# x's two halves, the weights' VectorE steps and row 0 put at other places of the attention loop of a fused attention and two-layer kernel

## The chip, the core and the metric

One core of a Trainium2 chip runs the whole kernel as one program. Its engines work side by side, each on its own queue of instructions, strictly in the order in which they were written: TensorE (PE, with its weight loads as PEld), VectorE (DVE), ScalarE (ACT), GpSimd (POOL) and SyncE (SP), which issues the loads. They wait for one another through semaphores. The metric is the device time of one execution in microseconds; lower is better.

## The reference

```python
def _attn_ref(q, k, v):
    scores = scale * np.matmul(q, k.transpose(0, 1, 3, 2))
    scores = np.where(mask, -1000000000.0, scores)
    scores = scores - np.max(scores, axis=-1, keepdims=True)
    attn = np.exp(scores)
    attn = attn / (np.sum(attn, axis=-1, keepdims=True) + 1e-09)
    return np.matmul(attn, v).astype(np.float32)
...
x = np.ascontiguousarray(attn_out.transpose(0, 2, 1, 3)).reshape(B * S, H * D)
x = _moe_ref(x=x, **moe_kwargs)          # (sigmoid(x @ w_gate) * (x @ w_val)) @ w_out
return _moe2_ref(x=x, **moe2_kwargs)     # h = x @ w_in; (h * cos(h)) @ w_out
```

Causal attention with 2 batches, 12 heads, 448 positions and 64 columns per head; then two dense layers on 896 tokens of 768 columns, with 1536 and 2048 inner columns. The weights come as 64-bit floats, and the kernel makes 32-bit words of them on the chip.

## The kernel before

**Precision.** Each operand of the dense layers is kept as a high part and a low part (the rest), and a product is made of three matmuls: high by high, high by low, low by high. A high part is a ScalarE copy, the low part a VectorE subtraction behind it.

**The attention loop** runs over 12 pairs of heads, t = 0 to 11, and is a pipeline over three or four iterations. In iteration t stand, in the order in which they are written:

- `scores(t)`: for each of seven rows of 64 positions, in `ORDER = (0, 2, 1, 3, 4, 6, 5)`, the score matmuls on TensorE (L328) into a bank of PSUM, a score step on VectorE that masks and takes the extreme (L334, with a short read of its accumulator), and an exponential on ScalarE (L338) that also sums. The widths are 64 to 448 columns; the last row in this order has 384. At the end, from iteration 3 on, `next(preparing)` puts one step of the first weight chunk behind: `prepare()` makes the words (L182 on ScalarE, L184 on VectorE) and the high and low part (L193 on ScalarE, L195 on VectorE) in halves of 384 columns. VectorE's four steps of it fall into iterations 7, 8, 10 and 11, ScalarE's into 4, 5, 9 and 10.
- `attend(t - 2, t - 3)`: products with the values (L379), the first half for pair t - 2, the second for t - 3, whose x is then complete in PSUM.
- `transposes(t - 1, iteration(t))`: 14 transposes of the scaled exponentials (L353) in four groups g = 0 to 3, each into a bank and from there to SBUF by a copy of rows: groups 0 and 2 by VectorE (L360), 1 and 3 by ScalarE (L358). `iteration(t)` gives a hook, `before(g)`, that is called ahead of each copy.

**In the hook** stand, for the iterations from 3 on: ahead of the copy of group 1 the high part of x of pair t - 3 (`split_x(t - 3, 0)`, L392, ScalarE); ahead of that of group 2 `normalise(t)`: the reciprocals of the sums (`invert`, L297 and L298, VectorE) and the scaling of the seven rows by POOL (`scale`, L307), row 0 first; ahead of that of group 3 the low part of x (`split_x(t - 3, 1)`, L395, VectorE, from PSUM and the high part) and POOL's addition of both parts (L396). VectorE executes an iteration therefore as: seven score steps, weight step if there is one, first copy, reciprocals, second copy, low part of x.

**What sets the order.** The schedule is manual: the order in which the lines run is the order on each engine. PSUM has eight banks that all these tiles share, so the score matmuls of an iteration wait for the exponentials, copies and x's low part of the iteration before, whose banks they take over. The scaled rows live in three buffers.

**Behind the loop** the first dense product (L245 to L247) is woven with the last products and transposes; a full weight step of 768 columns (`decode_chunk`) and the high and low parts of x of pairs 9 to 11 stand there. The dense layers follow (L562 to L564 and others) until the end.

Of the kernel before, what the change touches and what calls it, by code (L numbers as in the profile page):

```python
# [10 lines left out]
F32 = mybir.dt.float32  # L11
# [7 lines left out]
ALU = mybir.AluOpType  # L19
# [4 lines left out]
NPAIR = H // 2  # L24
NQT = S // D
# [57 lines left out]
def attn_moe_moe2(  # L83
# [9 lines left out]
    nc = tc.nc  # L93
# [13 lines left out]
    def bank():  # L107
        return psum.tile([P, 512], F32, tag="ps", name="ps")
# [8 lines left out]
    XB = [[None] * KX for b in range(B)]  # L117
# [83 lines left out]
    def decode_chunk():  # L201
        c = step("decode")
        if c is not None:
            singles[c] = Chunk(c)
            for n in range(2):
                singles[c].decode(n, 0, singles[c].n)
# [11 lines left out]
    def prepare():  # L218

        step("split")  # L220
        k = Chunk(step("decode"))
        a, b = (0, k.n // 2), (k.n // 2, k.n)
        for todo in (
            [], [(k.decode, 0, a)], [(k.decode, 0, b)], [], [(k.decode, 1, a)],
            [(k.decode, 1, b)], [(k.split, 0, a)],
            [(k.split, 1, a), (k.split, 0, b)], [(k.split, 1, b)],
        ):
            for do, n, cols in todo:
                do(n, *cols)
            yield  # L230

    def decode_load():
        decode_chunk()
# [6 lines left out]
    def products(ps, wt, rhs, first, last, ks=None):  # L240
        hi, lo = wt
        n = len(rhs)
        for k in ks or range(n):
            r, blk = rhs[k], slice(k * P, k * P + P)
            mm(ps[:, :S], lhsT=hi[:, blk], rhs=r[:, 0], start=first and k == 0, stop=False)  # L245
            mm(ps[:, :S], lhsT=hi[:, blk], rhs=r[:, 1], start=False, stop=False)  # L246
            mm(ps[:, :S], lhsT=lo[:, blk], rhs=r[:, 0], start=False, stop=last and k == n - 1)  # L247
# [5 lines left out]
    with tc.tile_pool(name="apool", bufs=1) as apool, tc.tile_pool(name="a2", bufs=2) as a2:  # L253
# [46 lines left out]
        def scale(t, rows, engine):  # L300
            pb, (sums, rs) = pbuf[t % 3], soft[t]
            for i in rows:
                row, by = pb[:, POFF[i] : POFF[i] + D * (i + 1)], rs[:, i : i + 1]
                if engine is nc.scalar:
                    nc.scalar.activation(row, row, AF.Copy, scale=by)
                else:
                    engine.tensor_scalar(row, row, by, 1.0, op0=ALU.mult, op1=ALU.mult)  # L307

        def normalise(t, i0, i1):
            invert(t, i0, i1)  # L310
            scale(t, range(i0, i1), nc.gpsimd)

        def scores(t):

            blocks = at.pop(t).rearrange("p (n c) -> p n c", c=QKW)
            pb = pbuf[t % 3]
            nm = a2.tile([P, 8], F32, tag="nm", name="nm")
            sums = a2.tile([P, 8], F32, tag="sums", name="sums")
            soft[t] = sums, a2.tile([P, 8], F32, tag="rs", name="rs")
            for n, i in enumerate(ORDER):  # L320
                w = D * (i + 1)
                ps = bank()
                for h in range(2):
                    rows = slice(h * D, h * D + D)
                    o, k0 = ((1 - h) * D, 2 * D) if i in CROSSED else (h * D, D)
                    parts = ((i, i + 1, 0), (0, i, D)) if i == TURNED else ((0, i + 1, 0),)
                    for n0, n1, c in parts:
                        mm(  # L328
                            ps[o : o + D, c : c + (n1 - n0) * D], lhsT=blocks[rows, i, :D],
                            rhs=blocks[rows, n0:n1, k0 : k0 + D], start=n0 == parts[0][0], stop=True,  # L330
                            skip_group_check=True,
                        )
                m0 = S - D if i == TURNED else S - w
                nc.vector.tensor_tensor_reduce(  # L334
                    out=ps[:, :w], in0=ps[:, :w], in1=mask[:, m0 : m0 + w], scale=-0.125, scalar=3.0e38,
                    op0=ALU.add, op1=ALU.min, accum_out=nm[:, i : i + 1],
                )
                nc.scalar.activation(  # L338
                    pb[:, POFF[i] : POFF[i] + w], ps[:, :w], AF.Exp, scale=-1.0,
                    bias=nm[:, i : i + 1], accum_out=sums[:, i : i + 1],  # L340
                )
                if (t, n) in ROWS_BEHIND:
                    normalise(*ROWS_BEHIND[t, n])
            next(preparing, None)
# [43 lines left out]
        def split_x(t, part):  # L388
            b, p = divmod(t, NPAIR)
            x = XB[b][p]  # L390
            if part == 0:
                nc.scalar.activation(x[:, 0], xps[t][:, :S], AF.Copy)  # L392
            else:
                xf = x.bitcast(F32)
                nc.vector.tensor_tensor(x[:, 1], xps.pop(t)[:, :S], xf[:, 0], op=ALU.subtract)  # L395
                nc.gpsimd.tensor_tensor(X32[p][:, b], xf[:, 0], xf[:, 1], op=ALU.add)  # L396

        def iteration(t):

            def before(g):  # L400
                if g == 1 and t >= 3:
                    split_x(t - 3, 0)
                if t == 1 and g > 1:
                    normalise(1, *((0, 4), (4, NQT))[g - 2])
                if 1 < t < NP - 1 and g == 2:
                    normalise(t, 0, NQT)
                if t == NP - 1 and g == 2:
                    invert(t, 0, NQT)
                    scale(t, (1, 2, 3), nc.gpsimd)
                if t >= 3 and g == 3:  # L410
                    split_x(t - 3, 1)
            return before


# [4 lines left out]
        for t in range(NP):  # L419
            if t == 3:  # L420
                preparing = prepare()
            scores(t)
            if t + 3 < NP:
                load_attn(t + 3, (nc.sync,) * 2, [(0, VOFF)] if t else [(0, 4 * QKW), (4 * QKW, VOFF)])
            if t >= 2:
                attend(t - 2, *([t - 3] if t > 2 else []))
            if t + 3 < NP:
                load_values(t + 3)
            if t >= 1:
                transposes(t - 1, iteration(t))  # L430
            if t == NP - 1:
                scale(t, (4, 5), nc.scalar)
                scale(t, (6, 0), nc.vector)
            if t in (1, 2, 9):
                load_chunk()
# [3 lines left out]
        xr = [[XB[b][k] for k in KORD] for b in range(B)]  # L439
        products(pg[0], wt, xr[0], True, False, range(0, 2))  # L440
        attend(NP - 2, NP - 3)
        decode_chunk()
        transposes(NP - 1, iteration(NP))
        products(pg[0], wt, xr[0], False, False, range(2, 4))
# [2 lines left out]
        nc.scalar.copy(fence, xps[NP - 1][:, D : D + 1])  # L447
        split_x(NP - 2, 0)
        split_x(NP - 2, 1)
        products(pg[0], wt, xr[0], False, True, range(4, KX))  # L450
        attend(NP - 1)
        split_x(NP - 1, 0)
        split_x(NP - 1, 1)
        pg.append(bank())
        products(pg[1], wt, xr[1], True, True)

# [858 lines left out]
```

## Time and profile before

| what | us |
|---|---|
| median of 3 runs | 526.16 (526.01 to 526.53) |
| the profiled execution's own time | 525.88 |
| its span, first to last instruction | 524.1 |
| TensorE busy | 518.0 |
| VectorE busy | 433.5 |
| ScalarE busy | 354.7 |
| POOL busy | 57.4 |

The granted TensorE clock was 0.999 of full speed over the span. A busy time is the sum of an engine's instructions, with waits left out, but a matmul's end is modelled, so TensorE's busy share says little about its pace. The views that the next sections use are the timeline of an engine (start and length of each instruction, in us from the start of the span, and in brackets the idle time ahead of it with what ended it) and tables of groups of instructions.

### The profile page before, as it was taken

What the parts mean: (1) busy time and instruction counts of PE and PEld (TensorE: products, weight loads), DVE (VectorE), ACT (ScalarE), POOL (GpSimd) and SP (SyncE); (2) the same over time, 40 slices, a digit from 0 to 9 for tenths busy, and PEclk for the clock granted to TensorE, in tenths of its full rate; (3) what the DMA queues carried; (4) which work ended last, traced back from release to release, by engine and by line L of the source; (5) the groups of instructions that cost most, each with busy time, mean ns of one, the idle gap of its engine ahead of it and who ended that gap; (6) DMA issues with size and microseconds to landing.
All of it is one profiled execution on the core that took longest, in us unless ns stands there. A gap on an engine that the chain in (4) does not pass through costs nothing.

```text
span 524.1 us, 8771 instructions
## 1 busy us (share of the span) xinstructions
PE 518.0 (99%) x3252; PEld 469.3 (90%) x3252; DVE 433.5 (83%) x823; ACT 354.7 (68%) x694; POOL 57.4 (11%) x111
## 2 busy tenths in 40 slices
PE   8999999999999999999999999999999999999997
PEld 6776789999999999999999999999999999999996
DVE  7889969987777899988865779998899878896883
ACT  7998965675555676776645557776687967874550
POOL 5787740000000000000000000000000000000111
PEclk9999999999999999999999999999999999999999
DMA  8966014354444433323342413444333333353422
GB/s 300 393 209 218 2 61 131 111 165 137 127 127 132 135 120 123 120 83 121 88 154 82 159 61 120 128 151 143 123 121 100 104 98 101 100 161 120 157 88 88
DMA packets 15658, 68.98 MB, mean 132 GB/s; under 512 B 1824, under 2 KB 2848, under 8 KB 15616
## 3 DMA queue, kind: packets, MB, share of 16 engines
q1 hardware_dynamic: 14688, 65.72, 38.4%
q0 software_dynamic: 640, 2.29, 1.2%
q8 instruction: 25, 0.41, 0.3%
q10 hardware_dynamic: 288, 0.41, 0.2%
q14 instruction: 17, 0.14, 0.1%
HBM read 65.67 MB, written 2.75 MB: 131 GB/s over the span
## 4 chain that ended last, share of the span: by engine, by line
PE 86%; DVE 5%; ACT 5%; issue 3%; POOL 1%; DMA 0%; DVEq 0%; POOLq 0%; ACTq 0%
PE ps L563 18%; PE ps L564 18%; PE ps L562 18%; PE ps L245 8%; PE ps L247 8%; PE ps L246 8%; ACT pbuf L338 3%; PE ps L379 2%; PE ps L328 2%; PE ps L353 2%; DVE wf L184 1%; DVE ps L334 1%; PE ps L275 1%; ACT up L182 1%; DVE wlo L475 1%
## 5 line engine op out<-in xcount | busy, mean ns | idle before, releaser
L182 ACT ACTIVATE up<-wraw 128x768 f16<-128x768 bf16 (+2 forms) x71 | 74.2, 1045 | 0.0
L184 DVE SCALAR_TENSOR_TENSOR wf<-wraw,up 128x768 uint32<-128x768 uint32 (+2 forms) x71 | 68.2, 961 | 7.1 <-ACT up L182 5.4
L563 PE MATMUL ps<-T,whi 128*128 128x448 f32 x189 | 68.6, 363 | 0.0
L562 PE MATMUL ps<-T,whi 128*128 128x448 f32 x189 | 68.5, 363 | 0.0
L564 PE MATMUL ps<-T,wlo 128*128 128x448 f32 x189 | 68.2, 361 | 0.0
L529 ACT ACTIVATE whi<-s 128x768 fp32r<-128x768 f32 x46 | 38.9, 845 | 39.0 <-DVE s L475 38.9
L475 DVE TENSOR_TENSOR wlo<-s,whi 128x768 fp32r<-128x768 f32 x46 | 43.9, 955 | 12.2 <-ACT whi L529 11.6
L1170 POOL DMA_DIRECT2D out_dram<-sg x8 | 4.5, 568 | 430.3 <-DVE sg L1169 430.3
L245 PE MATMUL ps<-g,whi 128*128 128x448 f32 x120 | 43.6, 363 | 0.0
L247 PE MATMUL ps<-g,wlo 128*128 128x448 f32 x120 | 43.5, 362 | 0.0
L246 PE MATMUL ps<-g,whi 128*128 128x448 f32 x120 | 43.2, 360 | 0.0
L338 ACT ACTIVATE pbuf<-ps,nm 128x64 f32<-128x64 f32 (+6 forms) x84 | 38.6, 476 | 6.5 <-POOL pbuf L307 3.5
L307 POOL TENSOR_SCALAR pbuf<-pbuf,rs 128x192 f32<-128x192 f32 (+6 forms) x80 | 36.6, 480 | 18.6 <-DVE rs L298 12.5
L562 PEld LDWEIGHTS ps<-T,whi 128*128 128x128 f32 x189 | 35.5, 188 | 2.9 <-issue 0.2
L564 PEld LDWEIGHTS ps<-T,wlo 128*128 128x128 f32 x189 | 35.4, 187 | 2.6 <-DVE wlo L475 0.2
L563 PEld LDWEIGHTS ps<-T,whi 128*128 128x128 f32 x189 | 35.5, 188 | 2.0
L195 DVE TENSOR_TENSOR wlo<-wf,whi 128x768 fp32r<-128x768 f32 (+2 forms) x22 | 20.9, 950 | 17.3 <-ACT whi L193 17.2
L334 DVE CUSTOM_DVE_ANT_0 ps<-ps,mask 128x64 f32<-128x64 f32 (+6 forms) x84 | 32.7, 457 | 2.7 <-PE ps L328 2.7
L563 PE MATMUL ps<-x,whi 128*128 128x448 f32 x90 | 32.7, 363 | 0.0
L562 PE MATMUL ps<-x,whi 128*128 128x448 f32 x90 | 32.6, 362 | 0.0
L564 PE MATMUL ps<-x,wlo 128*128 128x448 f32 x90 | 32.5, 361 | 0.0
L475 DVE TENSOR_TENSOR wlo<-wf,whi 128x768 fp32r<-128x768 f32 x26 | 24.8, 952 | 4.7 <-ACT whi L529 4.5
(152 smaller groups left out, 1374.6 us busy)
## 6 DMA issues: line engine op xcount, KB each, us to landing
wraw<-in_w_gv_dram SPq DMA_DIRECT2D x24, 768.0 KB, 4.4
wraw<-in_w_out_dram SPq DMA_DIRECT2D x24, 768.0 KB, 4.4
wraw<-in_w_in_dram SPq DMA_DIRECT2D x16, 768.0 KB, 4.3
qk<-in_qkv_dram SPq DMA_DIRECT2D x8, 672.0 KB, 4.6
v<-in_qkv_dram SPq DMA_DIRECT2D x12, 320.0 KB, 6.0
wraw<-in_w_out_dram SPq DMA_DIRECT2D x6, 512.0 KB, 3.7
out_dram<-sg POOLq DMA_DIRECT2D x8, 224.0 KB, 2.2
qk<-in_qkv_dram SPq DMA_DIRECT2D x4, 288.0 KB, 4.9
```

The costliest lines, as they stand in the source:

```text
L182: nc.scalar.activation(up.bitcast(F16)[:, 1::2], self.top[:, e0:e1], AF.Copy)
L184: nc.vector.scalar_tensor_tensor(self.w[:, e0:e1].bitcast(U32), self.mid[:, e0:e1], 13, up.bitcast(U32), op0=ALU.logical_shift_right, op1= ...
L245: mm(ps[:, :S], lhsT=hi[:, blk], rhs=r[:, 0], start=first and k == 0, stop=False)
L246: mm(ps[:, :S], lhsT=hi[:, blk], rhs=r[:, 1], start=False, stop=False)
L247: mm(ps[:, :S], lhsT=lo[:, blk], rhs=r[:, 0], start=False, stop=last and k == n - 1)
L334: nc.vector.tensor_tensor_reduce(out=ps[:, :w], in0=ps[:, :w], in1=mask[:, m0 : m0 + w], scale=-0.125, scalar=3.0e38, op0=ALU.add, op1=ALU ...
L338: nc.scalar.activation(pb[:, POFF[i] : POFF[i] + w], ps[:, :w], AF.Exp, scale=-1.0, bias=nm[:, i : i + 1], accum_out=sums[:, i : i + 1],)
L475: nc.vector.tensor_tensor(dst, a, b, op=op)
L529: nc.scalar.activation(hi, src, AF.Copy)
L562: mm(ps[:, :S], lhsT=hi[:, blk], rhs=r[:, 0], start=start, stop=False, skip_group_check=True)
L563: mm(ps[:, :S], lhsT=hi[:, blk], rhs=r[:, 1], start=False, stop=False, skip_group_check=True)
L564: mm(ps[:, :S], lhsT=lo[:, blk], rhs=r[:, 0], start=False, stop=stop, skip_group_check=True)
```

## The change

The line numbers here are those of the changed kernel where rows of it are shown; L343 there is L338 before, L397 is L392, L400 is L395, L337 is L334, L363 and L365 are L358 and L360, L299 and L300 are L297 and L298, L307 and L309 are L305 and L307.

```diff
@@ prepare()
-            for do, n, cols in todo:
-                do(n, *cols)
-            yield
+            for engine in range(2):
+                for do, n, cols in todo:
+                    if n == engine:
+                        do(n, *cols)
+                yield
@@ normalise(t, i0, i1)
             invert(t, i0, i1)
-            scale(t, range(i0, i1), nc.gpsimd)
+            rows = list(range(i0, i1))
+            scale(t, rows[1:] + rows[:1] if len(rows) == NQT else rows, nc.gpsimd)
@@ scores(t), behind the score step
+                if n == NQT - 1:
+                    yield
                 nc.scalar.activation(
@@ split_x, and a new function
                 nc.vector.tensor_tensor(x[:, 1], xps.pop(t)[:, :S], xf[:, 0], op=ALU.subtract)
-                nc.gpsimd.tensor_tensor(X32[p][:, b], xf[:, 0], xf[:, 1], op=ALU.add)
+
+        def whole_x(t):
+            b, p = divmod(t, NPAIR)
+            xf = XB[b][p].bitcast(F32)
+            nc.gpsimd.tensor_tensor(X32[p][:, b], xf[:, 0], xf[:, 1], op=ALU.add)
@@ before(g)
-                if g == 1 and t >= 3:
-                    split_x(t - 3, 0)
+                if g == 0 and t >= 3:
+                    split_x(t - 3, 1)
+                if g == 2:
+                    next(preparing, None)
...
-                if t >= 3 and g == 3:
-                    split_x(t - 3, 1)
+                if g == 3 and t >= 3:
+                    whole_x(t - 3)
@@ the loop over pairs
-            scores(t)
+            tiles = scores(t)
+            next(tiles)
...
+            if t >= 3:
+                split_x(t - 3, 0)
+            next(tiles, None)
@@ behind the loop
             attend(NP - 2, NP - 3)
+        split_x(NP - 3, 0)
         decode_chunk()
...
         split_x(NP - 2, 1)
+        whole_x(NP - 2)
...
         split_x(NP - 1, 1)
+        whole_x(NP - 1)
```

The same instructions are issued, in another order. On ScalarE x's high part stands ahead of the pair's last exponential (384 columns) instead of behind it. ScalarE in iteration 7 before, where `x` is x of pair 4 and `pbuf` holds the exponentials:

```order
L338 ACTIVATE pbuf_99,sums<-ps,nm 128x320
L338 ACTIVATE pbuf_99,sums<-ps,nm 128x448
L338 ACTIVATE pbuf_99,sums<-ps,nm 128x384
L392 ACTIVATE x_71<-ps 128x448
L358 COPY pt<-ps 128x512 x2
```

and now:

```order
L343 ACTIVATE pbuf_99,sums<-ps,nm 128x320
L343 ACTIVATE pbuf_99,sums<-ps,nm 128x448
L397 ACTIVATE x_71<-ps 128x448
L343 ACTIVATE pbuf_99,sums<-ps,nm 128x384
L363 COPY pt<-ps 128x512 x2
```

The high part and the last exponential have changed places. VectorE in the same iteration before, from the last score step to the next pair's first (`ISA` rows are the score steps and the reads of their accumulator):

```order
L334 ISA ps,nm<-ps,mask 128x384
L334 ISA nm 128x1
L184 SCALAR_TENSOR_TENSOR wf_424<-wraw,up 128x384
L360 COPY pt<-ps 128x384
L297 TENSOR_SCALAR sums<-sums 128x7
L298 RECIPROCAL rs<-sums 128x7
L360 COPY pt<-ps 128x384
L395 TENSOR_TENSOR x_71<-ps,x_71 128x448
L334 ISA ps,nm<-ps,mask 128x64
```

and now:

```order
L337 ISA ps,nm<-ps,mask 128x384
L337 ISA nm 128x1
L400 TENSOR_TENSOR x_71<-ps,x_71 128x448
L365 COPY pt<-ps 128x384
L184 SCALAR_TENSOR_TENSOR wf_446<-wraw,up 128x384
L299 TENSOR_SCALAR sums<-sums 128x7
L300 RECIPROCAL rs<-sums 128x7
L365 COPY pt<-ps 128x384
L337 ISA ps,nm<-ps,mask 128x64
```

The low part of x has moved from the end of the iteration to directly behind the score steps, and the weight step from ahead of the first copy to behind it. Behind the loop, ScalarE before (`x_76` is x of pair 9, L182 with 768 columns the full weight step, L305 the scaling of two rows of the last pair):

```order
L358 COPY pt<-ps 128x512 x2
L305 ACTIVATE pbuf_100<-pbuf_100,rs 128x320
L305 ACTIVATE pbuf_100<-pbuf_100,rs 128x384
L182 ACTIVATE up<-wraw 128x768
L392 ACTIVATE x_76<-ps 128x448
L358 COPY pt<-ps 128x512 x2
```

and now:

```order
L363 COPY pt<-ps 128x512 x2
L307 ACTIVATE pbuf_100<-pbuf_100,rs 128x320
L307 ACTIVATE pbuf_100<-pbuf_100,rs 128x384
L397 ACTIVATE x_76<-ps 128x448
L182 ACTIVATE up<-wraw 128x768
L363 COPY pt<-ps 128x512 x2
```

The full weight step has changed places with the high part of x of pair 9. On POOL, row 0 of each pair from 2 to 10 is scaled last instead of first, and the addition of x stays behind the scaling.

## Rows read from the trace of the kernel before

**Rows 1.** The page, busy time and share of the span by engine.

```profile
PE 518.0 (99%) x3252; PEld 469.3 (90%) x3252; DVE 433.5 (83%) x823; ACT 354.7 (68%) x694; POOL 57.4 (11%) x111
```

**Rows 2.** Busy time by stretch: stretch, its length, engines (count), clock, DMA share, GB/s.

```profile
16.20:64.20 48.00, 47.27 (x738) 34.43 (x738) 44.25 (x173) 43.74 (x158) 37.57 (x71) 1.00 0.56 198
...
80.00:500.00 420.00, 420.00 (x2099) 392.70 (x2098) 352.13 (x554) 281.47 (x465) 1.83 (x3) 1.00 0.38 122
```

**Rows 3.** Timeline of PE, iterations 7 and 8: start, length, line, count.

```profile
37.20 1.80 PE L328 MATMUL ps<-qk 64*64 64x64 f32 x32
38.77 1.76 PE L379 MATMUL ps<-pt,v 64*64 64x384 f32 x36
...
42.13 2.54 PE L328 MATMUL ps<-qk 64*64 64x64 f32 x32
```

**Rows 4.** Timeline of DVE: pair 3's first score step, then iteration 6's end.

```profile
17.03 0.22 DVE L334 CUSTOM_DVE_ANT_0 ps<-ps,mask 128x64 f32<-128x64 f32 x1
...
36.10 0.56 DVE L360 COPY pt<-ps 128x384 f32<-128x384 f32 x1 [0.60 <-PE ps L353]
36.58 0.16 DVE L297 TENSOR_SCALAR sums<-sums 128x7 f32<-128x7 f32 x1
...
36.96 0.51 DVE L360 COPY pt<-ps 128x384 f32<-128x384 f32 x1
37.38 0.61 DVE L395 TENSOR_TENSOR x<-ps,x 128x448 fp32r<-128x448 f32 x1
37.91 0.22 DVE L334 CUSTOM_DVE_ANT_0 ps<-ps,mask 128x64 f32<-128x64 f32 x1
```

**Rows 5.** Timeline of DVE: iteration 7's weight step and copy, iteration 11's low part.

```profile
40.54 1.39 DVE L184 SCALAR_TENSOR_TENSOR wf<-wraw,up 128x384 uint32<-128x384 uint32 x1
41.85 0.55 DVE L360 COPY pt<-ps 128x384 f32<-128x384 f32 x1
...
65.39 0.61 DVE L395 TENSOR_TENSOR x<-ps,x 128x448 fp32r<-128x448 f32 x1
```

**Rows 6.** Timeline of ACT: iteration 3's last exponential, then iteration 7.

```profile
20.23 0.58 ACT L338 ACTIVATE pbuf<-ps,nm 128x384 f32<-128x384 f32 x1
...
38.31 0.31 ACT L338 ACTIVATE pbuf<-ps,nm 128x64 f32<-128x64 f32 x1 [0.42 <-POOL pbuf L307]
...
40.91 0.60 ACT L338 ACTIVATE pbuf<-ps,nm 128x384 f32<-128x384 f32 x1
...
41.47 0.57 ACT L392 ACTIVATE x<-ps 128x448 fp32r<-128x448 f32 x1
```

**Rows 7.** Timeline of POOL around iteration 7: scaling, then the add of x.

```profile
37.21 3.20 POOL L307 TENSOR_SCALAR pbuf<-pbuf,rs 128x64 f32<-128x64 f32 x7 [0.89 <-DVE rs L298]
40.37 1.15 POOL L396 TENSOR_TENSOR xf<-x 128x448 f32<-128x448 f32 x1
```

**Rows 8.** Timelines of ACT and DVE: x's parts of pair 10, behind the loop.

```profile
72.01 0.55 ACT L392 ACTIVATE x<-ps 128x448 fp32r<-128x448 f32 x1
...
72.59 0.62 DVE L395 TENSOR_TENSOR x<-ps,x 128x448 fp32r<-128x448 f32 x1 [0.51 <-ACT x L392]
```

**Rows 9.** Groups on DVE in the dense stage (count, busy, mean ns), then L395's (min/median/max).

```profile
L184 DVE SCALAR_TENSOR_TENSOR wf<-wraw,up 128x768 uint32<-128x768 uint32 x58 | 55.5, 956 | 5.9 <-ACT up L182 4.2
...
L475 DVE TENSOR_TENSOR s<-s,wf 128x384 f32<-128x384 f32 x22 | 12.3, 558 | 0.8
...
L395 DVE TENSOR_TENSOR x<-ps,x x12: 608/615/626, 21.8 to 75.6; 128x448 fp32r<-128x448 f32 x12
```

**Rows 10.** Timelines of PEld and ACT behind the loop: products' weight loads, weight step, high part.

```profile
65.98 0.15 PEld L379 LDWEIGHTS ps<-pt,v 64*64 64x64 f32 x4 [0.17 <-issue]
...
70.17 0.21 PEld L379 LDWEIGHTS ps<-pt,v 64*64 64x64 f32 x8 [0.30 <-issue]
...
66.13 1.08 ACT L182 ACTIVATE up<-wraw 128x768 f16<-128x768 bf16 x1
67.42 0.54 ACT L392 ACTIVATE x<-ps 128x448 fp32r<-128x448 f32 x1 [0.21 <-PE ps L379]
```

## The prediction

> **What bounds the kernel now.** I read the page's busy line first: TensorE is at work nearly all the time [rows 1]. Then the table by stretches, to learn where it is not at its pace: from 80 to 500 us there are 2099 matmuls in 420.00 us, 0.2001 us each, so that stage is TensorE's alone, and a delay that reaches its start is carried to the end unshortened [rows 2]. In the attention loop no engine has that pace: VectorE is busy for 44.25 of 48.00 us and ScalarE for 43.74. TensorE's own need is seen in the least disturbed iteration, 37.20 to 42.13, 4.93 us from one pair's scores to the next [rows 3]; nine such would be 44.4 us, and the loop's nine take 48.0. So I followed VectorE through one iteration. T is the start of a pair's first score step (L334).
>
> Without a weight step [rows 4]: first copy of rows to the next step 0.48 us (36.10 to 36.58), invert 0.38 (to 36.96), second copy 0.42 (to 37.38), x's low part 0.53 (to 37.91). The seven score steps take 2.63 us (37.91 to 40.54, [rows 4, 5]). That is 4.44 us of work; what is left of such an iteration is waiting, for TensorE's transposes above all (0.60 before 36.10). With a weight step VectorE has no wait: 1.31 us (40.54 to 41.85) come on top [rows 5]. From T of pair 3, 17.03, to the end of the second copy of iteration 11, 65.39, there are 48.36 us [rows 4, 5]. Nine times 4.44, four times 1.31, less the one low part that lies behind 65.39, is 44.67: 3.69 us are waiting.
>
> **ScalarE beside it.** In the iteration with T = 37.91 the first exponential starts at 38.31, T + 0.40, the seventh at 40.91, T + 3.00, and x's high part at 41.47 [rows 6]. ScalarE needs 2.60 us for six exponentials and has no gap between them, so it is 0.4 us or more behind VectorE when the last score step ends. Now this costs nothing, since VectorE asks for the high part only after both copies.
>
> **The change part by part.** *x's two halves.* No instruction is added. The high part now starts behind the sixth exponential, at T + 3.00. Its time to the start of the low part is 0.58 us when VectorE is waiting (72.01 to 72.59, [rows 8]). The low part is now the first thing behind the last score step, so VectorE stands from T + 2.63 to T + 3.58: a new wait of 0.95 us in each of the nine iterations 3 to 11. Queued behind it on VectorE are the first copy, the weight step, the reciprocals, the second copy and the next pair's score steps; behind those wait ScalarE's exponentials, POOL's scaling and the score matmuls that want the banks. In iteration 3 the seventh exponential began at T + 3.20 [rows 6], so there it is 1.15. TensorE's second product of the pair, which the high part needs too, is no limit: it starts when the pair's last score matmul is done and needs some 1.7 us (1.76 from 38.77 in iteration 7, [rows 3]), before T + 3.00. The wait is a loop on VectorE's own queue (score steps, six exponentials, high, low, copies, score steps), and no buffer shortens it. The old waits of 3.69 us lie inside the new ones: the transposes are through before VectorE gets to its copy at T + 4.11.
>
> *The low part's own price.* It reads one operand from PSUM and one from SBUF. All twelve now take 608 to 626 ns, beside POOL's scaling or with POOL idle [rows 9], a slot of 0.53 us. In its new place it stands beside POOL's add of x (L396), which no row shows. The bounds are 0.53 us, if the add doesn't hold it, and 1.05, if it waits for the add's end (about T + 4.15, by the working of the next part) and then runs its 0.48 us. I take 0.53, because its rows are like that under POOL's other instructions.
>
> *The weight steps.* Four of them, 384 columns wide. POOL's add ran from 40.37 for 1.15 us, to 41.52; the weight step issued at 40.54 ended at 41.93, 0.41 us behind the add, and took 1.39 us [rows 5, 7]. The same width of a step with two operands in SBUF takes 0.558 us in the dense stage, where POOL is idle [rows 9]. So the add holds the weight step. In the new place POOL has been through by then: its scaling starts when the reciprocals are there, 0.63 us behind the first copy (37.21 against 36.58) and so 0.17 us ahead of the next T, takes 3.16 us to the add (37.21 to 40.37, [rows 7]), and the add ends near T + 4.15. The weight step follows the first copy at T + 4.59. Its slot is then 0.558 less the 0.08 us by which an operation overlaps the next, 0.48 instead of 1.31: 0.83 us won four times, 3.3 us. The cover is 0.44 us; if it is gone the old 1.31 stands, and that is the upper bound.
>
> The SBUF — State Buffer page of the Trainium skill (Who interferes with whom) says that a VectorE instruction with two SBUF inputs contends with a GpSimd instruction that reads SBUF, and one with at most one SBUF input does not. The weight steps agree (1.39 against 0.56 us); for the low part beside the add no run here shows it. By that rule the sum below stands, and by the weight step's row applied to the low part it would be the 533.6 of the rivals.
>
> *Reciprocals, row 0, the SP queue.* POOL's scaling comes later by about 0.5 us against T and takes as long; TensorE needs its first three rows first, and has the last by T + 3.1, ahead of VectorE's second copy at T + 4.97. Row 0 last (the 64-wide one) changes only which row is ready when, inside that slack. ScalarE's weight steps stay where they were. The loads of a later pair are issued at the same release of their buffers. I cost these at nothing.
>
> **The sum in the loop.** An iteration: 3.58 + 0.53 + 0.48 + 0.38 + 0.42 = 5.39 us; with a weight step 5.87. From 17.03 to the end of the second copy of iteration 11: 5.59 (iteration 3) + 4 x 5.39 + 4 x 5.87 = 50.63, against 48.36: 2.27 us later. Put the other way: 8.75 us of new wait, less 3.69 old, less 3.32 of the hold, plus the 0.53 of the low part that now lies inside.
>
> **The sum behind the loop.** TensorE had 0.45 us of slack there: the second piece of its product ran at 65.98, the copy it needs was through 0.09 us behind 65.39, with some 0.05 to be seen. So it is late by 2.27 - 0.45 = 1.82. Then ScalarE's order bites: x's high part of pair 9 waited until 67.42 for TensorE, and the full weight step (66.13) stood ahead of it [rows 10]; now it stands behind. High part at 69.24, weight step at 69.67 (0.54 less an overlap of 0.11) for 1.08, VectorE's half of it at 70.78 for 0.87 (0.956 less the overlap, POOL idle, [rows 9]), low part 0.53, first copy 0.55: 72.73. The product that needs this copy ran at 70.17 [rows 10], so it is late by about 2.6, and its second piece, which needs the second copy, by about 2.7. Nothing behind it has to wait longer than before. The whole: **2.7 us**.
>
> The profiled execution took 525.88 us with a span of 524.1; 2.7 more is 528.6. The median of the runs shown is 526.16, 0.28 above, so I say **528.9 us**.
>
> **The rivals.** *Faster: the low part fills VectorE's wait.* If the high part were there when the last score step ends, VectorE would have 4.44 us, or 4.92 with a free weight step, and the loop would run at TensorE's 4.93: eight iterations and the piece of the ninth are 39.4 + 4.9 = 44.3 us against 48.36, some 4 us less, 522.1. What speaks for it are the old waits of 0.60 us; against it, ScalarE's unbroken row of exponentials. It turns at the new wait's size: each 0.1 us of it is 0.9 us of time, so 0.65 us in place of 0.95 gives no change, and below 0.53 it is faster by over 0.2%. Chance 0.08, and 0.11 for a wait between 0.53 and 0.77, which can't be told from no change (0.2%, about 1.05 us, is what a measurement can tell).
>
> *POOL holds the low part.* The add meets the low part in nine iterations, 0.52 us each: 4.7 us more, 533.6. Chance 0.07.
>
> *The weight step is still held.* If POOL's add is later than worked out by 0.44 us, up to 0.83 us comes back in four iterations: up to 532.2. Chance 0.08.
>
> *The change moves less than it says,* the same order on the engines: excluded by the order of instructions printed above.
>
> **Chances and range.** The forecast has 0.66 (528.0 to 529.8). With the two held cases slower is 0.81, within 0.2% 0.11, faster 0.08. The range runs from 526.8, inside the case of no change, to 532.3, past the held weight step; the free loop and the held low part are left out.
>
> **What would show it.** The trace of the changed kernel should show VectorE idle for 0.9 to 1.0 us before each low part of x, released by ScalarE's high part; T to T of 5.4 us without and 5.9 with a weight step; weight steps of 0.56 us in place of 1.39; low parts still of 0.61; no idle before VectorE's first copy; and the dense stage shifted by 2.7 us and no longer than before. I am wrong if the idle time before the low part is under 0.7 us, if low parts take 1.1 us, or if the dense stage's own length changes.

## The result, and the profile after

| what | before | after |
|---|---|---|
| median, us | 526.09 (525.85 to 526.53, 6 runs) | 528.99 (528.84 to 529.71, 6 runs) |
| the profiled execution's own time | 525.88 | 528.84 |
| its span | 524.1 | 527.0 |

The changed kernel is slower by 2.9 us: the ratio is 1.0057, with a 95% interval of 1.0044 to 1.0070. The forecast was 528.9.

The dense stage first. This is the row of the table by stretches that answers to the second of [rows 2].

```profile
80.00:500.00 420.00, 420.00 (x2099) 392.74 (x2098) 352.97 (x554) 281.39 (x465) 2.29 (x4) 1.00 0.38 121
```

It holds 2099 matmuls in 420.00 us, as before: that stage has kept its pace, and the time was lost ahead of it. So here is VectorE in iteration 7, from the last score steps to the next pair's first (the reads of the accumulator are left out). It answers to [rows 4] and [rows 5].

```profile
39.24 0.22 DVE L337 CUSTOM_DVE_ANT_0 ps<-ps,mask 128x64 f32<-128x64 f32 x1
...
41.35 0.60 DVE L337 CUSTOM_DVE_ANT_0 ps<-ps,mask 128x384 f32<-128x384 f32 x1
...
42.84 0.62 DVE L400 TENSOR_TENSOR x<-ps,x 128x448 fp32r<-128x448 f32 x1 [0.83 <-ACT x L397]
43.39 0.55 DVE L365 COPY pt<-ps 128x384 f32<-128x384 f32 x1
43.85 0.55 DVE L184 SCALAR_TENSOR_TENSOR wf<-wraw,up 128x384 uint32<-128x384 uint32 x1
44.32 0.17 DVE L299 TENSOR_SCALAR sums<-sums 128x7 f32<-128x7 f32 x1
44.58 0.20 DVE L300 RECIPROCAL rs<-sums 128x7 f32<-128x7 f32 x1
44.70 0.51 DVE L365 COPY pt<-ps 128x384 f32<-128x384 f32 x1
45.12 0.22 DVE L337 CUSTOM_DVE_ANT_0 ps<-ps,mask 128x64 f32<-128x64 f32 x1
```

With T = 39.24, the low part starts at T + 3.60, behind 0.83 us of idleness that ScalarE's high part ends; the copy follows at T + 4.15 without a wait, the weight step at T + 4.61 takes 0.55 us instead of 1.39, and the next pair starts at T + 5.88. ScalarE in the same iteration, with the last two exponentials and the high part between them, shows where the wait comes from ([rows 6] before):

```profile
41.63 0.66 ACT L343 ACTIVATE pbuf<-ps,nm 128x448 f32<-128x448 f32 x1
42.15 0.23 ACT L343 ACTIVATION_READ_ACCUMULATOR pbuf<-ps,nm 128x1 f32 x1
42.24 0.57 ACT L397 ACTIVATE x<-ps 128x448 fp32r<-128x448 f32 x1
42.66 0.62 ACT L343 ACTIVATE pbuf<-ps,nm 128x384 f32<-128x384 f32 x1
```

The high part starts at T + 3.00, straight behind the sixth exponential. POOL beside it ([rows 7] before): scaling, then the add of x.

```profile
39.07 3.20 POOL L309 TENSOR_SCALAR pbuf<-pbuf,rs 128x128 f32<-128x128 f32 x7 [1.11 <-ACT pt L363]
42.23 1.14 POOL L405 TENSOR_TENSOR xf<-x 128x448 f32<-128x448 f32 x1
```

The add runs from 42.23 to 43.37. The low part (42.84) lies inside that and takes its 0.62 us; the weight step (43.85) comes 0.48 us behind it. The same for all nine iterations, in VectorE's groups between 17.39 and 68.25 (count, busy us and mean ns, idle us ahead with what ended it):

```profile
L365 DVE COPY pt<-ps 128x384 f32<-128x384 f32 x19 | 10.0, 526 | 0.0
...
L400 DVE TENSOR_TENSOR x<-ps,x 128x448 fp32r<-128x448 f32 x9 | 5.6, 625 | 7.7 <-ACT x L397 7.7
...
L195 DVE TENSOR_TENSOR wlo<-wf,whi 128x384 fp32r<-128x384 f32 x2 | 1.1, 550 | 0.0
L184 DVE SCALAR_TENSOR_TENSOR wf<-wraw,up 128x384 uint32<-128x384 uint32 x2 | 1.1, 549 | 0.0
```

7.7 us of idleness ahead of nine low parts is 0.86 each. The 0.95 of the forecast is counted from where the accumulator read behind the last score step begins (41.87 in iteration 7), and that read takes 0.14 us; counted like that the wait is 0.97 in iteration 7. None is left ahead of the copies. From one pair's first score step to the next there are 5.59 us in iteration 3, 5.42 in iterations 4 to 6 and 9, and 5.88, 5.89, 5.94 and 5.88 in the four that have a weight step (7, 8, 10 and 11, the last one to the end of its second copy).

Behind the loop, TensorE's weight loads of the products before (the second piece of the product whose first piece is the 70.17 of [rows 10]), then the same loads now, ScalarE and VectorE:

```profile
70.55 0.15 PEld L379 LDWEIGHTS ps<-pt,v 64*64 64x64 f32 x4 [0.17 <-ACT whi L193]
```

```profile
68.45 1.00 PEld L384 LDWEIGHTS ps<-pt,v 64*64 64x64 f32 x28 [0.46 <-issue]
...
73.21 0.24 PEld L384 LDWEIGHTS ps<-pt,v 64*64 64x64 f32 x8 [1.10 <-ACT whi L193]
73.72 1.14 PEld L384 LDWEIGHTS ps<-pt,v 64*64 64x64 f32 x28 [0.27 <-issue]
```

```profile
69.64 0.55 ACT L397 ACTIVATE x<-ps 128x448 fp32r<-128x448 f32 x1 [0.57 <-PE ps L384]
70.08 1.07 ACT L182 ACTIVATE up<-wraw 128x768 f16<-128x768 bf16 x1
71.02 1.06 ACT L363 COPY pt<-ps 128x512 f32<-128x512 f32 x2
72.18 0.84 ACT L193 ACTIVATE whi<-wf 128x768 fp32r<-128x768 f32 x1
```

```profile
71.18 0.96 DVE L184 SCALAR_TENSOR_TENSOR wf<-wraw,up 128x768 uint32<-128x768 uint32 x1 [2.15 <-ACT up L182]
72.06 0.62 DVE L400 TENSOR_TENSOR x<-ps,x 128x448 fp32r<-128x448 f32 x1
72.59 1.01 DVE L365 COPY pt<-ps 128x384 f32<-128x384 f32 x2
```

The high part of pair 9 waits 0.57 us for TensorE with the full weight step behind it. VectorE stands 2.15 us for that step and does its own half, the low part and the copies after it, and the next product stands 1.10 us until 0.62 us behind the start of the first of these copies (the bracket names ScalarE's L193, which ends about then, at 73.02).

### The profile page after: what moved, and what is told of

Its sections match the earlier page's. It is cut to its first block, busy times and chain, and to the rows that moved or that the text cites. A ratio compares the mean times of both kernels' runs of the same rounds, so it can differ in the third digit from the quotient of the medians.

```text
span 527.0 us, 8743 instructions
## 1 busy us (share of the span) xinstructions
PE 520.7 (99%) x3252; PEld 470.4 (89%) x3252; DVE 429.7 (82%) x823; ACT 354.8 (67%) x694; POOL 57.4 (11%) x111
## 3 DMA queue, kind: packets, MB, share of 16 engines
HBM read 65.67 MB, written 2.75 MB: 130 GB/s over the span
## 4 chain that ended last, share of the span: by engine, by line
PE 92%; DVE 3%; issue 2%; ACT 2%; POOL 1%; DMA 0%; POOLq 0%; ACTq 0%
PE ps L581 18%; PE ps L580 18%; PE ps L582 18%; PE ps L247 8%; PE ps L249 8%; PE ps L248 8%; PE ps L331 4%; PE ps L384 4%; PE ps L358 3%; DVE wf L184 1%; ACT up L182 1%; PE ps L277 1%; DVE wlo L493 1%; DMA out_dram<-sg 0%; DVE s L493 0%
## 5 line engine op out<-in xcount | busy, mean ns | idle before, releaser
L182 ACT ACTIVATE up<-wraw 128x768 f16<-128x768 bf16 (+2 forms) x71 | 74.2, 1045 | 0.0
L184 DVE SCALAR_TENSOR_TENSOR wf<-wraw,up 128x768 uint32<-128x768 uint32 (+2 forms) x71 | 66.3, 933 | 8.7 <-ACT up L182 7.0
L343 ACT ACTIVATE pbuf<-ps,nm 128x64 f32<-128x64 f32 (+6 forms) x84 | 39.1, 480 | 8.6 <-DVE nm L337 8.4
L309 POOL TENSOR_SCALAR pbuf<-pbuf,rs 128x64 f32<-128x64 f32 (+6 forms) x80 | 36.6, 478 | 21.4 <-DVE rs L300 10.0
L337 DVE CUSTOM_DVE_ANT_0 ps<-ps,mask 128x64 f32<-128x64 f32 (+6 forms) x84 | 32.7, 458 | 2.9 <-PE ps L331 2.9
L195 DVE TENSOR_TENSOR wlo<-wf,whi 128x768 fp32r<-128x768 f32 (+2 forms) x22 | 18.9, 860 | 16.9 <-ACT whi L193 16.8
```

The costliest lines, as they stand in the source:

```text
L182: nc.scalar.activation(up.bitcast(F16)[:, 1::2], self.top[:, e0:e1], AF.Copy)
L184: nc.vector.scalar_tensor_tensor(self.w[:, e0:e1].bitcast(U32), self.mid[:, e0:e1], 13, up.bitcast(U32), op0=ALU.logical_shift_right, op1= ...
L343: nc.scalar.activation(pb[:, POFF[i] : POFF[i] + w], ps[:, :w], AF.Exp, scale=-1.0, bias=nm[:, i : i + 1], accum_out=sums[:, i : i + 1],)
```

## The experiments

All times of the traces below are counted from T of pair 3, the first score step of iteration 3, because the stretch ahead of it differs between executions (see the second profile of the kernel before, further down). "Loop" is the time from there to the end of the second copy of iteration 11 (taken, as in the prediction, 0.42 us behind the copy's start, where VectorE's next step could begin), "product" the time to the second piece of the product behind the loop (73.72 in the rows above, so 56.33; 70.55 before, so 53.52). The last column is what the clock says of whole runs against those of the kernel before on the same chip.

| kernel | loop, us | product, us | against before, from the trace | between medians |
|---|---|---|---|---|
| before | 48.36 | 53.52 | | |
| after | 50.86 | 56.33 | +2.81 | +2.90 |
| weight steps alone | 47.40 | 52.91 | -0.61 | -0.69 |
| x's halves alone | 48.86 | 54.82 | +1.30 | +1.47 |
| low part behind the first copy | 47.71 | 53.64 | +0.12 | -0.18 |
| high part ahead of two exponentials | 49.93 | 55.75 | +2.23 | +2.21 |
| full weight step first, behind the loop | 50.86 | 55.56 | +2.04 | +2.34 |
| POOL's add first | 57.21 | 62.69 | +9.17 | +9.26 |
| low part behind the copy and full weight step first | 47.75 | 52.69 | -0.83 | -0.78 |
| row 0 first | 50.80 | 56.27 | +2.75 | +2.39 |

The two last columns agree to within 0.4 us in each row. From that product to the end of the span there are between 453.2 and 453.6 us in every one of these profiles. So what the change costs is decided between pair 3 and that product, and what lies behind it gives back or adds no more than about 0.4 us.

### The two parts apart

The weight steps alone: x's halves where they were before, VectorE's weight step behind the first copy, row 0 last. Against the kernel before:

```diff
@@ prepare()
-            for do, n, cols in todo:
-                do(n, *cols)
-            yield
+            for engine in range(2):
+                for do, n, cols in todo:
+                    if n == engine:
+                        do(n, *cols)
+                yield
@@ normalise(t, i0, i1)
-            scale(t, range(i0, i1), nc.gpsimd)
+            rows = list(range(i0, i1))
+            scale(t, rows[1:] + rows[:1] if len(rows) == NQT else rows, nc.gpsimd)
@@ before(g)
+                if g == 2:
+                    next(preparing, None)
```

> The weight steps behind the first copy and row 0 last, x's halves where they were before. Theory (the wait for x's high part costs 8.8 us, the weight steps give back up to 3.3): no wait for the high part; POOL's add still ends 3.6 us after a pair's first score step, so the weight step is held for part of its time (0.6 to 1.0 us instead of 1.39) and hides behind the first copy; iterations with a weight step 5.3 us instead of 5.73: 524.4 to 525.4 us. Rival (the later reciprocals and row 0 last are what makes the change slower): over 527.5.

Measured: 525.59 us, ratio 0.9987 (0.9978 to 0.9997), 0.2 us above the upper end of the expectation and faster than before. VectorE in its iteration 7:

```profile
40.35 0.60 DVE L337 CUSTOM_DVE_ANT_0 ps<-ps,mask 128x384 f32<-128x384 f32 x1
...
41.36 0.56 DVE L363 COPY pt<-ps 128x384 f32<-128x384 f32 x1 [0.35 <-PE ps L356]
41.84 0.55 DVE L184 SCALAR_TENSOR_TENSOR wf<-wraw,up 128x384 uint32<-128x384 uint32 x1
```

The weight step has fallen from 1.39 to 0.55 us, but an iteration with one is only 0.33 us shorter (5.41 instead of 5.74): ahead of the first copy stand now 0.35 us in which VectorE waits for TensorE's transposes. The hold had covered them. The hold of 0.6 to 1.0 us that was still expected did not come, but only just: POOL's add ends at 41.83 and the weight step starts at 41.84. In iteration 10 that wait is 0.65 us and nothing is won (5.73 against 5.69). Of the 3.3 us of VectorE's work that the move takes away, the loop keeps 0.96.

x's halves alone: the weight step at its old place behind the score steps, now directly ahead of the low part. Against the kernel after:

```diff
@@ prepare(), before(g), normalise(t)
-            for engine in range(2):
-                for do, n, cols in todo:
-                    if n == engine:
-                        do(n, *cols)
-                yield
+            for do, n, cols in todo:
+                do(n, *cols)
+            yield
...
-                if g == 2:
-                    next(preparing, None)
...
-            scale(t, rows[1:] + rows[:1] if len(rows) == NQT else rows, nc.gpsimd)
+            scale(t, rows, nc.gpsimd)
```

> x's halves as in the change, the weight steps directly behind the score steps as before, row 0 first. Theory: the weight step stands inside the wait for the high part, so every iteration takes 5.4 us, with or without it: 5.6 + 8 x 5.39 = 48.7 us from pair 3's first score step to iteration 11's second copy, 2.2 less than in the changed kernel; with what lies behind the loop 526.4 to 527.3. Rival (POOL's scaling and add hold the weight step until the add's end at T + 4.15): the four iterations take 6.3 to 6.4 us, 530 to 531.

Measured: 527.75 us, ratio 1.0036 (1.0020 to 1.0052), above the expectation's upper end by 0.45 and 1.2 below the whole change. VectorE in iteration 7, then POOL there:

```profile
42.00 0.80 DVE L184 SCALAR_TENSOR_TENSOR wf<-wraw,up 128x384 uint32<-128x384 uint32 x1
42.97 0.62 DVE L398 TENSOR_TENSOR x<-ps,x 128x448 fp32r<-128x448 f32 x1 [0.17 <-ACT x L395]
43.51 0.55 DVE L363 COPY pt<-ps 128x384 f32<-128x384 f32 x1
```

```profile
39.20 3.19 POOL L307 TENSOR_SCALAR pbuf<-pbuf,rs 128x64 f32<-128x64 f32 x7 [1.11 <-ACT pt L361]
42.35 1.44 POOL L403 TENSOR_TENSOR xf<-x 128x448 f32<-128x448 f32 x1
```

The weight step lies in the time that VectorE would have stood for the high part, and the wait behind it shrinks to 0.17 us, although POOL's scaling makes the step 0.80 us long. All iterations from the fourth on are 5.40 or 5.41 us long, with a weight step or without. So in the presence of the wait, the weight step costs nothing where it was, and 0.47 us where the change has put it (5.89 against 5.42). In the loop the parts give -0.96 and +0.50 by themselves, and +2.50 together. Put the other way: beside the new wait, moving the weight steps does not win anything, it costs 2.00 us of the loop (50.86 against 48.86), four fifths of what the loop loses.

### The low part one place later

After, with the low part behind the first copy:

```diff
@@ before(g)
-                if g == 0 and t >= 3:
+                if g == 1 and t >= 3:
                     split_x(t - 3, 1)
```

> The changed kernel with x's low part behind the first copy of rows instead of ahead of it. Theory (the order low part, copy makes the wait): the copy fills 0.48 us of the wait, iterations 4.9 to 5.2 us without and 5.4 with a weight step, nine times some 0.45 us less than the changed kernel: 524.6 to 525.6. Rival (the wait for the high part isn't what sets the length, TensorE or POOL does): 528 or more.

Measured: 526.10 us, ratio 0.9997 (0.9987 to 1.0006). VectorE in iteration 7:

```profile
40.46 0.60 DVE L337 CUSTOM_DVE_ANT_0 ps<-ps,mask 128x384 f32<-128x384 f32 x1
...
41.47 0.56 DVE L365 COPY pt<-ps 128x384 f32<-128x384 f32 x1 [0.35 <-PE ps L358]
41.95 0.62 DVE L400 TENSOR_TENSOR x<-ps,x 128x448 fp32r<-128x448 f32 x1
```

No low part of the loop waits for ScalarE any more, and 3.15 of the loop's 50.86 us are gone. What VectorE waits for is TensorE's transposes again, 0.35 us here and up to 0.84. The size missed, by 0.5 us from the upper end of 524.6 to 525.6: some 0.45 us was expected from each of nine iterations, part of it went into those waits, and of the 3.15 us that the loop gained 2.69 are left at the product behind it (53.64 against 56.33). This run shows that the loss of the loop hangs on the place of this one instruction.

### The high part earlier

After, with x's high part ahead of the last two exponentials instead of the last one (from pair 3 on):

```diff
@@ scores(t)
+            held = []
+
+            def exponential(n, i, w, ps):
+                ...
@@ further down, behind the score step
-                if n == NQT - 1:
-                    yield
-                nc.scalar.activation(
...
+                if n < NQT - (2 if t >= 3 else 1):
+                    exponential(n, i, w, ps)
+                else:
+                    held.append((n, i, w, ps))
+            yield
+            for late in held:
+                exponential(*late)
```

`exponential` holds the activation and what stands behind it, as before.

> The changed kernel with x's high part ahead of the last two exponentials (448 and 384 columns) instead of the last, from pair 3 on. Theory (ScalarE's row of exponentials ahead of the high part sets the wait): the wait before the low part falls by 0.6 us, from 0.95 to 0.35, nine times; TensorE (4.93) and ScalarE (5.2 with its own weight step) then take over: 524.0 to 525.6. Rival (the high part waits for TensorE's product, not for the exponentials): the wait falls by less than 0.2 us, 527 or more.

Measured: 528.49 us, ratio 1.0039 (1.0023 to 1.0055). The time is the rival's; the theory's 524.0 to 525.6 is refuted. ScalarE in iteration 5 of this kernel, whose T is 28.19 (L326 is the exponential, L406 the high part, L393 TensorE's product), then the loads for some of that iteration's score matmuls, then VectorE's low parts in the loop:

```profile
30.14 0.57 ACT L326 ACTIVATE pbuf<-ps,nm 128x320 f32<-128x320 f32 x1
...
31.34 0.54 ACT L406 ACTIVATE x<-ps 128x448 fp32r<-128x448 f32 x1 [0.53 <-PE ps L393]
31.78 0.63 ACT L326 ACTIVATE pbuf<-ps,nm 128x448 f32<-128x448 f32 x1
```

```profile
28.34 0.32 PEld L341 LDWEIGHTS ps<-qk 64*64 64x64 f32 x12 [0.54 <-ACT pt L372]
```

```profile
L409 DVE TENSOR_TENSOR x<-ps,x 128x448 fp32r<-128x448 f32 x9 | 5.6, 625 | 5.9 <-ACT x L406 5.9
```

Here the high part could go at T + 2.6, but TensorE's product is not there until T + 3.15. ScalarE stands 0.53 us with two exponentials queued behind it, and VectorE's wait ahead of the low part is 0.96 us, longer than before. That is one of the bad iterations. In six of the nine the high part starts at T + 2.67 to 2.81 and the listed wait is 0.47 to 0.61 us; in iterations 5, 6 and 10 it is 0.90 to 0.96. Over all nine the wait falls from 7.7 to 5.9 us, 0.2 us each, which is the bound of the rival, and the loop is 0.93 us shorter (49.93 against 50.86). The wait for the product is the rival's cause: in every iteration the high part starts within 0.1 us of the end of the product as the profile models it.

In the kernel after, that end lies at T + 2.6 to 2.7, 0.3 us or more ahead of the high part, so there the exponentials decide. Moved ahead, the high part can win about that much and no more. It wins less, because the exponentials behind it and ScalarE's copies come later: iterations 5, 6, 10 and 11 follow those with a ScalarE weight step, and in iteration 5 the score matmuls ahead of the product stand 0.54 us for ScalarE's copies. So the wait has a second cause close behind the first; a place between the two was not tried.

### Behind the loop

After, with ScalarE's full weight step ahead of the high part of pair 9 again:

```diff
@@ behind the loop
             attend(NP - 2, NP - 3)
-        split_x(NP - 3, 0)
         decode_chunk()
+        split_x(NP - 3, 0)
```

> The changed kernel with the full weight step ahead of the high part of x of pair 9 again, behind the loop. Theory (that swap costs 0.8 to 0.9 us of the 2.9): the product behind the last transposes no longer waits 0.75 us; 527.9 to 528.3. Rival (all of the difference is made in the loop): 528.8 to 529.2.

Measured: 528.64 us, ratio 1.0051 (1.0038 to 1.0063). Its weight load for the next product:

```profile
72.82 0.24 PEld L384 LDWEIGHTS ps<-pt,v 64*64 64x64 f32 x8 [0.33 <-issue]
73.33 1.14 PEld L384 LDWEIGHTS ps<-pt,v 64*64 64x64 f32 x28 [0.27 <-ACT whi L193]
```

Counted from T of pair 3 (17.77 here, 17.39 in the kernel after) the product's second piece runs at 55.56 instead of 56.33, 0.77 us earlier; the loop is as long as in the kernel after, 50.86. The medians lie 0.35 apart and the intervals overlap, so the gain is shown in the trace and not by the times; the median of 528.64 lies between the ranges of the theory and of the rival. By the trace ScalarE's swap costs 0.77 us.

### POOL's add first

The forecast's rival in which POOL holds VectorE had not come true. To see what a meeting would cost, POOL's add of x is put ahead of the scaling, so that it runs where VectorE does its weight step:

```diff
@@ before(g)
+                if g == 2 and t >= 3:
+                    whole_x(t - 3)
...
-                if g == 3 and t >= 3:
-                    whole_x(t - 3)
```

> The changed kernel with POOL's addition of x ahead of the scaling of the rows instead of behind it, so that the addition runs when VectorE comes to its weight step. Theory (POOL's addition holds a VectorE step with two operands in SBUF until its end): the four weight steps take 1.1 to 1.3 us instead of 0.55 and the kernel 531.0 to 532.0. Rival (the weight steps were long before for another reason): steps of 0.55 us, 528.8 to 529.3.

Measured: 535.56 us, ratio 1.0183 (1.0167 to 1.0198), some 4 us more than expected. VectorE around two iterations, then POOL there, then VectorE's groups in the loop:

```profile
39.79 0.62 DVE L400 TENSOR_TENSOR x<-ps,x 128x448 fp32r<-128x448 f32 x1 [0.83 <-ACT x L397]
40.33 0.55 DVE L365 COPY pt<-ps 128x384 f32<-128x384 f32 x1
40.80 0.87 DVE L299 TENSOR_SCALAR sums<-sums 128x7 f32<-128x7 f32 x1
...
46.92 1.25 DVE L184 SCALAR_TENSOR_TENSOR wf<-wraw,up 128x384 uint32<-128x384 uint32 x1
48.10 0.16 DVE L299 TENSOR_SCALAR sums<-sums 128x7 f32<-128x7 f32 x1
```

```profile
40.50 1.14 POOL L405 TENSOR_TENSOR xf<-x 128x448 f32<-128x448 f32 x1 [1.34 <-DVE x L400]
...
46.63 1.14 POOL L405 TENSOR_TENSOR xf<-x 128x448 f32<-128x448 f32 x1 [1.34 <-DVE x L400]
```

```profile
L400 DVE TENSOR_TENSOR x<-ps,x 128x448 fp32r<-128x448 f32 x9 | 5.6, 625 | 7.7 <-ACT x L397 7.7
L299 DVE TENSOR_SCALAR sums<-sums 128x7 f32<-128x7 f32 x9 | 5.0, 551 | 0.0
```

The weight steps are held to 1.25 us, as expected. What the expectation lacked: in the five iterations without one the add holds the next instruction in line, a TENSOR_SCALAR of seven columns, to 0.87 us instead of 0.16. So all nine iterations pay 0.7 us (6.12 instead of 5.42, 6.59 instead of 5.88 in iteration 7), and the loop is 6.35 us longer than in the kernel after (57.21 against 50.86). Copies from PSUM under the same add (40.33) keep their 0.55 us.

The SBUF — State Buffer page of the Trainium skill (Who interferes with whom) says that a tensor_scalar can, if its operands meet some conditions, run in a mode that takes the port pair which VectorE shares with GpSimd, and that the loser of that pair waits for the whole instruction. The trace agrees: 0.87 us, with its end (41.67) just behind the add's (41.64). Had I used that sentence, the expectation would have had a hold in all nine iterations.

### Row 0, and the start of the kernel

After, with row 0 of a pair scaled first again:

```diff
@@ normalise(t)
-            scale(t, rows[1:] + rows[:1] if len(rows) == NQT else rows, nc.gpsimd)
+            scale(t, rows, nc.gpsimd)
```

> After with row 0 of a weight in its old place, ahead of the other rows, and all else as in after. Theory: the order of the rows inside a weight step decides nothing, since the consumers (TensorE's product and the copies' part on ScalarE) wait for the whole set of rows: 528.6 to 529.4, periods of an iteration 5.42 without and 5.88 with a weight step, as in after. Rival: row 0 last shortens or lengthens the chain by the one short step that stands ahead of the first copy: 0.1 to 0.2 us in each of the iterations, so 527.5 or 530.

Measured: 528.93 us, ratio 1.0045 (1.0029 to 1.0062), with a loop of 50.80 us against 50.86. Of these 0.06 us 0.05 lie in iteration 10, which takes 5.89 us here and 5.94 in the kernel after. Otherwise the place of row 0 decides nothing that can be seen.

And the kernel before once more, unchanged, with a second profile:

> The kernel before, unchanged, for a second profile. Theory (the later first score step of the changed kernel's profile, 4.63 against 4.43 us, and the 0.36 us at pair 3's are not the change's): a first score step anywhere from 4.4 to 4.7 and pair 3's from 17.0 to 17.6. Rival (the change starts the loop later): 4.43 and 17.03 again.

Measured: 526.44 us. The very first score step stands at 4.63, as in the kernel after. Pair 3's first score step, which stands at 17.03 in [rows 4], is here:

```profile
17.53 0.22 DVE L334 CUSTOM_DVE_ANT_0 ps<-ps,mask 128x64 f32<-128x64 f32 x1
```

From there to the end of the second copy of iteration 11 are 48.38 us (48.36 in the first profile), and to the product's second piece 53.57 (53.52). The loop repeats to hundredths, but it starts 0.5 us later in this execution. In the other kernels T of pair 3 lies between 17.24 and 17.77. So the 0.36 us by which the kernel after starts its loop later than [rows 4] lie inside what the start does by itself.

### A version that is faster than both

The two edits that each won something, the low part behind the first copy and the full weight step first behind the loop, together:

```diff
@@ before(g)
-                if g == 0 and t >= 3:
+                if g == 1 and t >= 3:
                     split_x(t - 3, 1)
@@ behind the loop
             attend(NP - 2, NP - 3)
-        split_x(NP - 3, 0)
         decode_chunk()
+        split_x(NP - 3, 0)
```

> The changed kernel with x's low part behind the first copy of rows and the full weight step ahead of pair 9's high part behind the loop: both repairs together. Theory (the two prices are independent): 526.1 less 0.8 to 0.9, 525.2 to 525.4, faster than both kernels. Rival (TensorE's slack behind the loop takes the second repair up): 525.9 to 526.2.

Measured: 525.52 us, ratio 0.9987 (0.9979 to 0.9996): 0.6 us below the low part's move alone, 3.5 below the changed kernel and 0.8 below the one before. That is 0.1 above the expectation. By the traces the second repair is worth 0.95 us of the product's time (52.69 against 53.64), about what was expected; the medians show 0.6 of it. The kernel ties with the weight steps alone (525.59), but in another way: its loop is 0.35 us longer (47.75 against 47.40), and the stretch from the loop to the product 0.57 us shorter. Both keep the weight step out of POOL's add and VectorE out of ScalarE's queue.

## Why the prediction came out as it did

*The new wait was right.* The high part starts at T + 3.00 and the low part at T + 3.60, forecast 3.00 and 3.58; in iteration 3 the low part comes at T + 3.78, as worked out. The listed idleness is 0.83 us in iteration 7, below the 0.9 to 1.0 that was said to show it, only because the read of the accumulator runs on into the gap. Putting the low part one place later takes the wait away, and 3.15 us of the loop with it.

*The old waits inside the new one* was right: 2.3 us stood ahead of the copies in the loop before, none do now. The runs without the wait got them back at once (4.1 us with the weight steps alone, 4.3 with the low part behind the copy).

*The low part's price* was right: 619 to 625 ns under POOL's add, so a slot of 0.54 to 0.55 us where 0.53 was taken. The rival in which POOL holds it is refuted. By the rule that the prediction cites from the Trainium skill (SBUF — State Buffer, Who interferes with whom), an instruction with at most one SBUF input does not contend, and the trace agrees for the low part. The page excepts the modes that use both ports of VectorE; the prediction leaves that exception out. It does not touch the low part, but by the page it is what the experiment with the add first ran into.

*The weight steps* were right in size: 0.55 us, 0.48 us clear of the add, where a cover of 0.44 was worked out. But "won four times, 3.3 us" was wrong as the worth of the move. Alone the move wins 0.96, since TensorE's transposes come next; and beside the new wait the step would have cost nothing at its old place, so that there the move loses 2.00. The prediction did not ask what the step would cost inside the wait that it had just worked out. The sum is not touched by that, because it counted the changed iteration instruction by instruction.

*The sum of the loop* was 0.23 us short: 2.50 against 2.27. Iteration 3 takes the 5.59 that were worked out. The four others without a weight step are 0.03 longer each (5.42 instead of 5.39): the handover takes 0.60 instead of the 0.58 of [rows 8] and the low part's slot 0.01 more. Of those with a weight step three are 0.01 to 0.02 longer than 5.87, and iteration 10 is 0.07 longer, with its high part at T + 3.06. That last bit is gone with row 0 first, a term that the prediction put at nothing.

*Behind the loop* the slack of 0.45 us was right: with ScalarE's old order the product is late by 2.04, which is 2.50 less 0.46. The chain that the prediction names is there: without the 0.36 by which this execution starts its loop later, the high part stands at 69.28 (forecast 69.24), VectorE's half of the weight step at 70.82 (70.78) and the product's first piece at 72.85 (72.73). The swap costs 0.77 where 0.8 to 0.9 was worked out. The errors of the loop and of the swap cancel for the most part: 2.81 in the trace against 2.7.

*The step from the trace to the median* is where luck may have helped. 0.28 us were added because the median of before stood above its profiled execution; the changed kernel's median stands 0.15 above its own. The start of the loop moves by half a microsecond between executions of one kernel, so the last 0.1 or 0.2 us of agreement show nothing.

*TensorE's product "no limit"* was right for this order, with 0.3 us or more to spare: one exponential earlier, and ScalarE waits for the product in six of nine iterations, for up to half a microsecond.

## What to carry to other kernels

A step that is moved ahead of others on an in-order engine is best put behind an instruction that doesn't need its input: here one place later turned a loss of 2.9 us into no change, because the copy then ran while the input was made. Cost the parts of a change with the others in place: work that is free inside a wait is paid in full once another part moves it out (here four weight steps, 2.00 us), and a wait that is taken away uncovers the next one, a third of a microsecond behind. Before ordering POOL's work, list what VectorE does in those microseconds, down to the instruction of seven columns.

## What the runs showed of the hardware

- POOL's add of two SBUF tensors held not only VectorE's steps with two SBUF operands (1.25 to 1.39 us instead of 0.55) but also a TENSOR_SCALAR with one SBUF tensor and seven columns, 0.87 us instead of 0.16. VectorE's low parts and copies, which read PSUM, were not held (0.62 and 0.55 us under the add).
- POOL's scaling, with one SBUF tensor, held a weight step too: with x's halves alone the step that was due at 42.00 ended at 42.80, 0.41 us behind the end of the scaling (42.39), and POOL's add, which started meanwhile, took 1.44 us instead of 1.14.
- The first 17 us, in which the first loads arrive, differed by half a microsecond between two executions of the same kernel (T of pair 3 at 17.03 and 17.53), while the 48 us behind them repeated within 0.02. A shift between two traces is better counted from an instruction behind that stretch.
